# A new hand-written order for a cosFormer attention and token-mixing kernel: most products of v on GpSimd, narrow tiles for k'v, twelve narrow q transposes

## The chip, the cores and the metric

The kernel runs on one core of one Trainium2 chip. Its metric is the device time of one execution, in microseconds (us); lower is better. TensorE multiplies matrices, VectorE, ScalarE and GpSimd work on elements, and SyncE's queue issues the transfers here. Each engine takes its own instructions strictly in order and waits on semaphores for the others.

## What is computed

Two stages, one behind the other, on 8 batches of 576 tokens with 8 heads of 64 columns. First a linear attention with cosine weights:

```python
theta = pi / 2 * pos / S
phi(x) = concat([relu(x) * cos(theta), relu(x) * sin(theta)])      # 64 -> 128 features
kv  = phi(k)^T v            # per head, 128 x 64
z   = sum over s of phi(k)
out = (phi(q) kv) / (phi(q) z + 1e-6)
```

Then, with the eight heads side by side as x (8 x 576 x 512), a mixing over tokens:

```python
wq, wk = x @ w_q, x @ w_k                # 512 -> 64
W_tok  = (wq wk^T) / sqrt(64)            # never built: wk^T x is formed first
result = relu(W_tok x) @ w_out           # 512 x 512
```

Inputs and the result are float32; the kernel works in bfloat16 and sums in float32. In and out are some 39 MB.

## The kernel before

The work is cut into 16 units H = 0 to 15, each a batch and half of its heads (four heads, two per row of 128 partitions); the four heads come as two halves "a" and "b". A batch b holds the units 2b and 2b+1, and a pair of batches fills nine output tiles of 128 rows, 36 tiles in all. The order of all work is one string of words, ORDER, which is read from left to right. Each word issues the instructions of one step on its engine; so for each engine the string fixes the order of its queue, and nothing else does. A letter behind @ names the engine (A ScalarE, V VectorE, G GpSimd), a number behind the colon the PSUM bank (of OE's tile also the output buffer).

The steps of one unit, with the lines of the profile:

- LK, LQ, LV (L145): load half a unit of k, q or v, 288 KB, into one of five raw buffers each.
- RK, RQ (L203, L205): relu of k and q to bfloat16, by halves or whole.
- The products of v with the two tables cos and sin, into one of two buffers "v2". There are two ways: CV (L209, L211), a cast of v to bfloat16 on any engine, and then VS (L234), the product on VectorE from SBUF; or VG (L248), the product on GpSimd straight from the raw float32.
- KV (k'v): per unit 36 matmuls on narrow tiles (L285: 64 rows, 64 columns of weights, 130 moving columns) or, for the units in KV_WIDE, 18 on wide ones (L275: 128 columns of weights, 260 moving). KE evicts the result.
- QT: the transposes of q, 9 wide ones of 128x128 (L295) for the units in QT_WIDE, else 18 narrow ones (L301). QM is the product of q with the tables on VectorE from PSUM: two instructions for a wide unit (L316), one for a narrow one (L320).
- N (L340): numerator and denominator, two steps per unit. EP adds 1e-6 to the denominator on ScalarE or VectorE (L357, L359); for the steps in EPS_PE two small matmuls do it (L348). RC or RJ is the reciprocal, X (L393) the division on VectorE.
- XT (L406, wide) or XR (L419, narrow): transposes of x; XE evicts them.

Then per batch WK, WQ, KX (L439, L452, L466) with their evictions KW, QW, XK, the copies XA and XB across partitions, four MX (L489) and ME (the relu, L500 or L502); per output tile WO (L509, four matmuls), OE (eviction to one of 16 buffers, L209 or L213) and ST (the store, L519). LW and CW load and cast the weights, WU is a few matmuls on constants.

Of the kernel before, what the change touches and what calls it, by code (L numbers as in the profile page):

```python
# [31 lines left out]
RC6 LQ4a KX0:4 X6 RK2@A QT2:2 RC7 X7 CV5@A KV2:0 LK7a XK0@V LV4a QM2 XB0@G QW0@A XT3:6 LV4b KE2@A
RK5@A LK4a VS5a N5:0 WU5:2 LK4b N4:2 VS5b XE3@A RQ5@G LV7a EP5@V KV5:4 RC5 RC4 X5 XA0@A LV7b X4
QT5:6 KE5@A RQ4@G LQ7b MX0:0 QM5 XR2:2 ME0@A LQ7a QT4:4 XE2@A LQ6a N10:0 QM4 MX1:6 CV4@G LK7b EP10@A
ME1@A WK1:2 LV6b WQ1:3 RC10 KW1@A VS4 RK4@A LQ6b KX1:2 MX2:6 LW2 N11:4 XK1@V QW1@A ME2@A EP11@V
KV4:2 LK6b RC11 XA1@G X10 CV7a@A CV7b@G LK6a X11 MX5:6 MX4:0 KE4@A RQ7b@G LV6a RQ7a@A VS7 N8:2 N9:4
ME5@A LV8a ME4@A QT7:6 RK7@G LW3 EP8@V EP9@V RJ4 RQ6a@A XT5:0 X8 LW4 XB1@G XE5@A X9 KV7:2 LW5 RQ6b@G
# [12 lines left out]
MX15:2 EP23@A KX4:5 RK10@A LV13b WQ4:0 XK4@V RQ13b@G RC23 WO3:1 ME15@A X23 XA4@G XB4@A QW4@A RQ12b@G  # L50
KV10:2 OE3:9@V RQ12a@A QT13:6 OE12:10@A VG12 MX18:0 WO14:5 QM13 KE10@A ST12 ME18@A LK13b XR11:2
OE14:11@A LK13a MX16:0 N21:6 XE11@V ME16@A LV14a N20:4 EP21@A EP20@V RK12@A QT12:0 RJ10 X21 WO16:2
RQ14b@A X20 WO13:3 QM12 VG13 XR10:4 OE13:10@A MX19:6 KV12:0 ME19@A ST13 WO17:3 OE16:12@A LK15b
KE12@V XE10@V LK14b MX17:0 LK14a OE17:13@A N25:6 ME17@V N24:4 LV15b RQ14a@A WK5:3 ST2 EP25@V EP24@V
RK13@A RJ12 QT14:0 X24 WO21:2 KW5@A X25 CV14a@G KV13:4 OE21:10@A QM14 CV14b@A WQ5:3 ST21 KE13@A
KX5:2 LQ15b VS14 LQ15a XR12:4 XK5@A N27:0 ST3 XE12@A N26:6 LK15a RK14a@G WO20:2 RC26 EP27@V RC27
XA5@G RK14b@A X27 WO19:4 XB5@G QW5@A VG15b X26 KV14:0 OE19:2@A MX21:6 KE14@A MX23:4 WO18:3 ME21@V
ME23@A OE20:10@V XR13:4 RQ15a@G MX22:6 RQ15b@V MX20:0 ST20 ME22@A WO15:2 VG15a ST17 XE13@V ME20@A
ST8 N28:6 OE18:9@V OE15:14@A ST9 N29:0 EP28@A QT15:4 RK15@A EP29@V RC28 WK6:3 RC29 X29 WO25:2 KW6@A
QM15 WQ6:3 OE25:15@A KV15:0 X28 QW6@A ST25 ST7 KX6:3 KE15@A ST15 N31:0 ST18 XR14:6 EP31@V N30:4 ST0  # L60
XE14@V WO23:2 EP30@A ST10 XK6@A RJ15 ST16 X30 XA6@G WO24:3 ST5 OE23:7@A XB6@G X31 WO26:2 OE24:0@A
# [9 lines left out]
def kernel(  # L71
# [126 lines left out]
    A, V, G = nc.scalar, nc.vector, nc.gpsimd  # L198
# [8 lines left out]
    def cast(eng, dst, s):  # L207
        if eng is A:
            A.copy(dst, s)  # L209
        elif eng is G:  # L210
            G.tensor_scalar(dst, s, 1.0, 1.0, op0=ALU.mult, op1=ALU.mult)  # L211
        else:
            V.tensor_copy(dst, s)  # L213
# [90 lines left out]
    def KE(H, ps, eng):  # L304
        if H in KV_WIDE:
            cast(eng, kv_b[H % 2][:, :, :, :, 0:D + 1],
                 kv_wide(place["KV", H]).rearrange("p r (q s e) -> p r q s e", q=2, s=2))
            return
        cast(eng, kv_b[H % 2][:, :, 0, :, 0:D + 1],
             kv_view(place["KV", H]).rearrange("p r (s e) -> p r s e", s=2))  # L310

    def QM(H, ps, eng):
        if H in QT_WIDE:
            q_t = qt_wide(place["QT", H]).rearrange("p c (r d) -> p r c d", r=2)
            for r in range(2):
                V.tensor_mul(  # L316
                    qm_b[H % NQM][:, :, r, 0:C, :],
                    q_t[:, r].unsqueeze(1).to_broadcast([P, 2, C, H2]), qtab)
# [13 lines left out]
    def N(g, ps, eng):  # L332
# [3 lines left out]
        for u in range(SC):  # L336
            for s in range(2):
                for pr in range(2):
                    a = slice(H2 * pr, H2 * pr + H2)
                    nc.tensor.matmul(  # L340
                        nv[:, pr, u, :], qm_b[H % NQM][a, s, r, 2 * u:2 * u + 2, :],
                        kv_b[H % 2][a, r, pr if H in KV_WIDE else 0, s, 0:D + 1],
                        start=(u == 0 and s == 0),
                        stop=(u == SC - 1 and s == 1 and g not in EPS_PE))
        if g in EPS_PE:
            for pr in range(2):
# [4 lines left out]
    def rec(g):  # L351
        return rec_b[g // 2 % 4][:, g % 2]
# [24 lines left out]
    def RC(g, ps, eng):  # L377
        V.reciprocal(rec(g), num(place["N", g])[:, :, :, D:D + 1] if g in EPS_PE else rec(g))

# [219 lines left out]
```

## Time and profile before

| | |
|---|---|
| median of three runs | 120.03 us (119.75 to 120.36) |
| profiled execution, first to last instruction (span) | 117.9 us |
| TensorE busy | 96.3 us, 82% |
| VectorE busy | 91.0 us, 77% |
| ScalarE busy | 82.7 us, 70% |
| GpSimd busy | 64.8 us, 55% |
| transfers | 39.38 MB, mean 334 GB/s |
| granted TensorE clock | 0.997 |

The profiled execution's own time is not given beside its span; the median of the runs lies 2.1 us above the span, which is what starts and ends around the first and last instruction. The engines' busy times are sums over stages with different limits. Matmuls are pipelined, so how long a step of TensorE keeps the queue is read from the distance of two starts or from the chain of waits rather than from its duration.

### The profile page before, as it was taken

The numbers are of one execution on the slowest core, as the hardware profiler recorded it, in microseconds if no ns is written. First come the engines' busy times: TensorE is split into PE (matmuls) and PEld (weight loads), VectorE is DVE, ScalarE is ACT, GpSimd is POOL, SyncE is SP. The second block draws the span as 40 slices with busy tenths as digits, with TensorE's granted clock in tenths as the row PEclk, the third lists the DMA queues.
The fourth block names the chain that finished last, engine by engine and source line by source line (L and its number), as shares of the span: only waits on it lengthen the run. The fifth ranks groups of instructions, "written<-read, shape, count | busy, mean of one in ns | idle before, by whom it ended". The sixth has DMA issues, their size and how long they took to land.

```text
span 117.9 us, 4967 instructions
## 1 busy us (share of the span) xinstructions
PE 96.3 (82%) x2109; PEld 65.3 (55%) x2109; DVE 91.0 (77%) x163; ACT 82.7 (70%) x146; POOL 64.8 (55%) x66
## 2 busy tenths in 40 slices
PE   0007866887897879998999889997999999999970
PEld 0006855756676768546966556654784566463420
DVE  2009799699899998989798887796997996794620
ACT  4555578489999797997684769975888783546340
POOL 7600599843435984584599972899549921102000
PEclk9999999999999999999999999999999999999998
DMA  3999999999999999999999899786989456999874
GB/s 95 353 389 408 393 363 351 391 389 396 385 393 389 391 385 387 389 395 384 387 381 341 271 317 379 274 253 215 299 285 321 171 205 268 402 343 402 340 306 172
DMA packets 20662, 39.38 MB, mean 334 GB/s; under 512 B 3232, under 2 KB 3232, under 8 KB 20640
## 3 DMA queue, kind: packets, MB, share of 16 engines
q1 hardware_dynamic: 20640, 39.07, 91.8%
q8 instruction: 16, 0.26, 1.0%
q14 instruction: 6, 0.05, 0.1%
HBM read 29.62 MB, written 9.44 MB: 331 GB/s over the span
## 4 chain that ended last, share of the span: by engine, by line
PE 46%; DMA 25%; DVE 9%; SPq 8%; ACT 4%; issue 3%; POOL 2%; POOLq 0%; DVEq 0%
PE ps L509 23%; DMA kraw<-in_k_dram 11%; DMA vraw<-in_v_dram 9%; SPq L145 8%; DMA qraw<-in_q_dram 5%; DVE qm L316 5%; PE ps L340 4%; PE ps L452 3%; PE ps L466 3%; PE ps L489 3%; PE ps L439 3%; PE ps L285 3%; PE ps L419 2%; PE ps L295 2%; POOL rq L205 2%
## 5 line engine op out<-in xcount | busy, mean ns | idle before, releaser
L248 POOL TENSOR_TENSOR v<-vraw,vtab 128x1152 bf16<-128x1152 f32 (+1 forms) x12 | 35.6, 2976 | 4.5 <-DVE qm L316 2.5
L509 PE MATMUL ps<-wow,mix 128*128 128x512 bf16 x144 | 34.6, 380 | 0.0
L393 DVE TENSOR_TENSOR x<-ps,rec 128x640 bf16<-128x640 f32 x32 | 25.4, 816 | 0.7
L209 ACT COPY o<-ps 128x512 f32<-128x512 f32 x25 | 14.6, 590 | 10.5 <-PE ps L509 9.2
L316 DVE TENSOR_TENSOR qm<-ps,qtab 128x1152 bf16<-128x1152 bf16 x28 | 19.7, 749 | 1.3 <-PE ps L295 1.2
L509 PEld LDWEIGHTS <-mix 128*128 128x128 bf16 x144 | 12.5, 98 | 14.5 <-issue 1.7
L295 PE MATMUL ps<-ident,rq 128*128 128x128 bf16 x126 | 10.3, 232 | 10.9 <-ACT rq L203 10.0
L234 DVE TENSOR_TENSOR v<-vb,vtab 128x2304 bf16<-128x2304 bf16 (+1 forms) x11 | 12.0, 1110 | 7.5 <-ACT vb L209 6.7
L500 ACT ACTIVATE mix<-ps 128x576 bf16<-128x576 f32 x23 | 14.5, 651 | 2.5 <-PE ps L489 2.3
L340 PE MATMUL ps<-kvs,qm 64*128 64x65 bf16 x640 | 14.0, 193 | 2.8 <-DVE qm L316 1.8
L340 PEld LDWEIGHTS <-qm 64*128 64x128 bf16 x640 | 12.6, 96 | 4.9 <-issue 3.3
L295 PEld LDWEIGHTS <-rq 128*128 128x128 bf16 x126 | 8.2, 104 | 12.5 <-issue 9.9
L203 ACT ACTIVATE rk<-kraw 128x1152 bf16<-128x1152 f32 (+1 forms) x14 | 13.9, 995 | 0.5 <-DMA kraw<-in_k_dram 0.3
L211 POOL TENSOR_SCALAR kx<-kx 64x256 bf16<-64x256 bf16 x10 | 4.0, 400 | 15.8 <-ACT kx L209 10.1
L205 POOL TENSOR_SCALAR rq<-qraw 128x576 bf16<-128x576 f32 (+1 forms) x13 | 10.1, 776 | 4.4 <-ACT rk L203 2.6
L211 POOL TENSOR_SCALAR vb<-vraw 128x576 bf16<-128x576 f32 (+1 forms) x7 | 5.7, 809 | 10.8 <-DMA vraw<-in_v_dram 9.5
L285 PE MATMUL ps<-v,rk 64*64 64x130 bf16 x432 | 9.1, 228 | 1.9 <-ACT mix L500 0.7
L209 ACT CAST kvs<-ps 128x260 bf16<-128x260 f32 (+1 forms) x15 | 6.5, 436 | 5.1 <-PE ps L285 3.8
L285 PEld LDWEIGHTS <-rk 64*64 64x64 bf16 x432 | 7.5, 112 | 4.3 <-ACT mix L500 1.3
L502 DVE TENSOR_SCALAR mix<-ps 128x576 bf16<-128x576 f32 x9 | 6.8, 753 | 3.3 <-PE ps L489 3.1
L213 DVE COPY xT<-ps 128x1280 bf16<-128x1280 bf16 (+1 forms) x9 | 7.3, 813 | 2.2 <-PE ps L419 2.0
L203 ACT ACTIVATE rq<-qraw 128x576 bf16<-128x576 f32 (+1 forms) x10 | 8.3, 830 | 0.9 <-DMA qraw<-in_q_dram 0.8
(65 smaller groups left out, 135.0 us busy)
## 6 DMA issues: line engine op xcount, KB each, us to landing
kraw<-in_k_dram SPq DMA_DIRECT2D x32, 288.0 KB, 5.9
qraw<-in_q_dram SPq DMA_DIRECT2D x32, 288.0 KB, 5.9
vraw<-in_v_dram SPq DMA_DIRECT2D x32, 288.0 KB, 5.9
out_dram<-o SPq DMA_DIRECT2D x36, 256.0 KB, 3.0
wof<-in_moe_w_out_dram SPq DMA_DIRECT2D x4, 256.0 KB, 5.7
wkf<-in_moe_w_k_dram SPq DMA_DIRECT2D x1, 128.0 KB, 6.7
wqf<-in_moe_w_q_dram SPq DMA_DIRECT2D x1, 128.0 KB, 6.5
```

Source lines behind the costliest of these rows:

```text
L203: A.activation(dst, s, AF.Relu)
L205: eng.tensor_scalar(dst, s, FMAX, 0.0, op0=ALU.min, op1=ALU.max)
L209: A.copy(dst, s)
L234: V.tensor_mul(v2_b[H % NV2][:, part, :, :, 0:D], vb_b[H % NPREP][:, part].unsqueeze(3).to_broadcast([P, n, C, 2, D]), vtab.unsqueeze(1).t ...
L248: G.tensor_mul(dst[:, part, :, :, 0:D], s[:, part].unsqueeze(3).to_broadcast([P, n, C, 2, D]), vtab.unsqueeze(1).to_broadcast([P, n, C, 2, ...
L285: nc.tensor.matmul(kv_v[o, r, :], rk_of(H)[a, pr, c, :], v2_b[H % NV2][a, pr, c, :, 0:D + 1], start=(c == 0), stop=(c == C - 1))
L295: nc.tensor.transpose(qt_v[:, c, :], rq_b[H % NPREP][:, c, :, :], ident)
L316: V.tensor_mul(qm_b[H % NQM][:, :, r, 0:C, :], q_t[:, r].unsqueeze(1).to_broadcast([P, 2, C, H2]), qtab)
L340: nc.tensor.matmul(nv[:, pr, u, :], qm_b[H % NQM][a, s, r, 2 * u:2 * u + 2, :], kv_b[H % 2][a, r, pr if H in KV_WIDE else 0, s, 0:D + 1], ...
L393: V.tensor_tensor(x_b[b % NX][:, :, 4 * h:4 * h + 4, :].rearrange("p u (w r) d -> p r w u d", r=2)[:, r], nv[:, :, :, 0:D], rec(g).to_broa ...
L500: A.activation(dst, s, AF.Relu, scale=scale_moe)
L509: nc.tensor.matmul(o, mix_b[bp % 2][:, m, rt * P:(rt + 1) * P], wow[:, m, :], start=(m == 0), stop=(m == NDM - 1))
```

## The change

The string ORDER is replaced as a whole, and three lists with it. The computation stays as it was. Counted over the kernel:

- products of v: VG goes from 9 half and 3 whole instructions to 21 half and 3 whole; VS from 5 half and 6 whole to 5 half and none. The casts CV go from 9 half and 4 whole to 5 half.
- KV: 72 wide matmuls and 432 narrow ones become 576 narrow ones.
- QT: wide units go from 14 to 4, narrow ones from 2 to 12.
- eps on TensorE: 5 steps become 10.
- relus: GpSimd 18 to 12 instructions, VectorE 4 to 1, ScalarE 24 to 43 (more of them halves).
- evictions move between ScalarE and VectorE in small numbers; loads, stores and output tiles are in another order.

The diff, cut to the lists and the first, a middle and the last lines of the string:

```diff
-LK1b TB TI LQ1a LQ0a TK LV1b TZ LV1a LK1a LQ1b TQ LQ0b LK0a RQ1a@G LV0a TW TV LV0b LK0b CV1@A LV3a
-LV3b VS1b RQ1b@A LQ3b VS1a T2 QT1:0 LQ3a RK1a@A RK1b@V RQ0@V LK3b KV1:2 QM1 LK3a QT0:4 KE1@A CV0@G
...
-OE2:2@A WO4:2 LK11a VS9 OE6:3@A LQ11a RK8b@A QT9:0 RK9a@G OE1:4@A WK3:3 LV11b QM9 QT8:4 RK9b@G KW3@A
-OE4:5@A KV8:0 QM8 XB2@A KV9:6 ST4 KE8@A LV12a MX9:4 KE9@A MX11:0 VG11a N16:2 ME9@A LK10a ME11@V
...
-OE35:4@A ST35 OE31:2@A ST31
+LV1a LV0b TK TQ LV0a TI TZ LV1b LQ1b LQ0a LQ1a LK1a T2 TV TB TW CV1a@A VG0b LK1b CV1b@A LQ0b RK1b@A
+VS1a RQ1@V WU14:0 LW0 RQ0a@A QT1:0 RQ0b@A LK0a LK0b VS1b RK1a@G VG0a KV1:2 QT0:4 LV3a LV2a LQ3a
...
+RQ9a@A QT9:0 OE4:6@A ME8@V RK9a@A QT8:2 RK8a@G KW3@V MX9:4 ME9@A WQ3:7 KX3:6 RK8b@A KV9:4 XK3@A
+KE9@A QM9 KV8:0 N19:4 RQ11b@A QM8 KE8@V N18:2 LV10a N16:0 EP16@V EP18@A EP19@V QW3@A WO7:6 RQ11a@A
...
+XB4@G MX13:4 RC22 ME13@A X22 N23:2 VG13a MX17:0 KE10@V N20:6 WO13:4 ME17@A EP23@V RC23 X23 EP20@V
...
+ST35 OE31:6@V ST32 OE33:10@A ST27 ST33 OE34:13@V ST31 ST34 WO28:6 OE28:0@A ST28
@@
-    EPS_PE = (3, 4, 14, 16, 26)
+    EPS_PE = (0, 1, 4, 5, 8, 9, 10, 14, 15, 25)
-    QT_WIDE = (0, 1, 2, 3, 4, 5, 6, 7, 8, 9, 10, 11, 12, 14)
-    KV_WIDE = (2, 4, 5, 7)
+    QT_WIDE = (0, 1, 2, 3)
+    KV_WIDE = ()
```

GpSimd's queue around the units 8 and 9, before. A row is line, operation, output, inputs and shape; "vraw" is a raw buffer of v, "v_84" and "v_85" the two buffers v2, "rk" and "rq" the relus, "x2" two rows alike (both halves):

```order
L205 TENSOR_SCALAR rq_80<-qraw_71 128x9x64
L205 TENSOR_SCALAR rk_78<-kraw_66 128x576
L205 TENSOR_SCALAR rq_81<-qraw_72 128x9x64 x2
L205 TENSOR_SCALAR rk_79<-kraw_67 128x576 x2
L248 TENSOR_TENSOR v_85<-vraw_74,vtab 128x18x64 x2
L205 TENSOR_SCALAR rq_80<-qraw_68 128x2x9x64
L248 TENSOR_TENSOR v_84<-vraw_73,vtab 128x18x64
```

The same place in the change ("vb" is a cast half of v, "kx" a copy across partitions):

```order
L211 TENSOR_SCALAR vb_83<-vraw_77 128x576
L248 TENSOR_TENSOR v_84<-vraw_76,vtab 128x18x64 x2
L248 TENSOR_TENSOR v_85<-vraw_77,vtab 128x18x64
L205 TENSOR_SCALAR rk_78<-kraw_66 128x576
L248 TENSOR_TENSOR v_85<-vraw_74,vtab 128x18x64 x2
L211 TENSOR_SCALAR kx_103<-kx_103 64x256
```

The relus of q and of pair 9's k have left GpSimd; in front of the one relu that stays (of k of unit 8) three half products of v have come in.

VectorE's queue ahead of the k'v of the units 8 and 9, before:

```order
L234 TENSOR_TENSOR v_84<-vb_82,vtab 128x36x64
L393 TENSOR_TENSOR x_95<-ps,rec_92 128x2x5x64
L502 TENSOR_SCALAR mix_105<-ps 128x576
L213 COPY xT_97<-ps 128x2x2x5x64
L234 TENSOR_TENSOR v_85<-vb_83,vtab 128x36x64
L316 TENSOR_TENSOR qm_87<-ps,qtab 128x2x576 x2
L316 TENSOR_TENSOR qm_86<-ps,qtab 128x2x576 x2
```

and in the change:

```order
L234 TENSOR_TENSOR v_85<-vb_83,vtab 128x18x64
L359 TENSOR_SCALAR rec_92<-ps 128x10 x2
L213 COPY o_107<-ps 128x512
L381 RECIPROCAL rec_92<-rec_92 128x20
L393 TENSOR_TENSOR x_95<-ps,rec_92 128x2x5x64 x2
L213 COPY o_109<-ps 128x512
L213 COPY o_110<-ps 128x512
L213 COPY xT_97<-ps 128x2x2x5x64
L502 TENSOR_SCALAR mix_105<-ps 128x576
L213 CAST wk_99<-ps 128x320
L320 TENSOR_TENSOR qm_87<-ps,qtab 128x4x576
L320 TENSOR_TENSOR qm_86<-ps,qtab 128x4x576
```

The two whole products of v are replaced by one half product, the two products of q per unit by one each, and three evictions of output tiles and one of wk have come in.

GpSimd's queue behind that place, in the change, up to its last product of v:

```order
L211 TENSOR_SCALAR kx_102<-kx_102 64x256 x2
L248 TENSOR_TENSOR v_85<-vraw_76,vtab 128x18x64
L248 TENSOR_TENSOR v_84<-vraw_75,vtab 128x36x64
L205 TENSOR_SCALAR rk_78<-kraw_65 128x576
L248 TENSOR_TENSOR v_85<-vraw_76,vtab 128x18x64
L248 TENSOR_TENSOR v_84<-vraw_77,vtab 128x36x64
L205 TENSOR_SCALAR rq_81<-qraw_68 128x2x9x64
L248 TENSOR_TENSOR v_85<-vraw_73,vtab 128x36x64
```

The two copies of batch 4 now stand ahead of the products for the units 12 to 15.

More of the change, by code (lines that the diff above doesn't have):

```diff
@@ L32 @@
[L32 to L37, printed above, removed]
@@ L50 @@
[L50 to L55, printed above, removed]
@@ L56 @@
[L56 to L61, printed above, removed]
@@ new lines @@
+RC4 VG4a LV7a RC5 LK7b X5 XT3:4 XA0@A XB0@A MX0:2 LQ7b LQ7a LV6b X4 QM5 LW2 LK6b LV6a XE3@V ME0@A
+MX1:6 RK5b@A RK5a@A LK6a XR2:2 MX3:0 ME1@A XE2@V KV5:4 LQ6b RQ4@A RK4b@G LQ6a MX2:6 WK1:2 KE5@A
+ME2@V KW1@V QT4:6 N11:4 LW3 VG7b RK4a@A ME3@A KV4:2 QM4 VG7a EP11@A RC11 N10:0 KE4@A X11 LW4 RC10
+N9:2 RC9 RK7a@A N8:6 RK7b@A RC8 VG6b VG6a KX1:4 WQ1:5 X9 XK1@A XB1@A X8 X10 LW5 XR4:6 LV9a QW1@A
+MX7:4 XR5:0 KV7:2 RQ7@A XA1@A XE4@V QT7:6 KE7@A ME7@A XE5@V MX4:0 RQ6a@G ME4@A WK2:2 QM7 LQ8b CW3@G
+LV8b MX5:4 MX6:0 LK9b KW2@A N14:6 N15:2 ME5@V RK6@A WQ2:4 RC14 CW4@G LV8a X14 LQ9b RQ6b@A KX2:5 RC15
@@ new lines @@
+RC18 OE7:7@A RC19 RC16 X19 VG11b WO12:7 WO0:6 X16 QT11:0 VG11a N17:4 X18 LQ10a XR9:2 XA3@A OE0:8@V
+OE12:9@A RK11b@A WO9:7 LK10a EP17@V RK11a@A LK12b WO11:6 LK10b LV12b RC17 LQ13b X17 KV11:4 QM11
+XB3@G LQ13a XE9@A OE9:10@A KE11@V XR8:2 OE11:11@A XE8@V LQ12b LV13a LV12a RQ10a@A LK13b RQ10b@A
+LQ12a MX15:6 VG10b MX12:0 VG10a WO10:4 WK4:5 LK13a ME12@A ME15@V QT10:6 RK10@G LK12a N22:0 RQ13b@G
+MX14:2 LQ14b OE10:12@A WQ4:4 KW4@A RQ13a@G KX4:5 ME14@A EP22@A QW4@A XK4@A XA4@G ST4 QM10 KV10:6
+XB4@G MX13:4 RC22 ME13@A X22 N23:2 VG13a MX17:0 KE10@V N20:6 WO13:4 ME17@A EP23@V RC23 X23 EP20@V
@@ new lines @@
+N21:0 MX16:2 WO17:5 RC20 EP21@V LQ14a LV13b RK12b@A RQ12b@A OE13:13@A RQ12a@A RC21 WO15:4 X21 ME16@A
+LK14b OE17:14@A XR11:0 X20 XR10:6 MX19:2 OE15:15@A ME19@A WO16:5 XE11@V VG12 QT13:2 QT12:0 RK13a@A
+XE10@V MX18:6 WK5:4 LV14b ST3 OE16:6@V RQ14b@A LV14a LK14a ME18@V RK12a@G QM12 WO19:5 LQ15a KW5@A
+OE19:0@A KV12:6 RQ14a@A LV15b KX5:4 KE12@A WQ5:5 N25:6 QM13 XK5@A RK13b@A QW5@V XB5@A N24:2 XA5@A
+RC25 QT14:4 VG13b ST2 KV13:0 EP24@A X25 KE13@A WO18:6 ST8 LQ15b WO21:7 QM14 N26:4 RC24 N27:0
+OE18:5@A ST10 LV15a ST1 X24 OE21:4@A XR12:2 ST6 LK15b EP26@V EP27@V RK14@A WO20:7 RJ13 XE12@A WO14:6
```

34 lines of the change are left out of this document (17 added, 17 removed).

## The prediction

> **What bounds the kernel now.** I read the stage windows first, then the chain of waits, then the groups of instructions with shapes kept apart. The stage windows (length; busy time of TensorE, its weight loads, VectorE, ScalarE and GpSimd with counts; granted clock; DMA share; GB/s):
>
> ```profile
> 9.60:25.10 15.50, 12.32 (x336) 10.14 (x336) 13.75 (x27) 9.77 (x17) 10.96 (x5) 1.00 1.06 380
> 25.10:56.00 30.90, 27.51 (x595) 20.44 (x596) 28.84 (x51) 27.60 (x48) 17.41 (x21) 1.00 1.05 390
> 56.00:96.70 40.70, 38.91 (x952) 25.62 (x953) 34.98 (x62) 31.15 (x59) 30.82 (x18) 1.00 0.87 297
> 96.70:114.30 17.60, 17.56 (x234) 9.08 (x232) 11.57 (x19) 8.13 (x17) 1.60 (x4) 1.00 0.88 334
> 114.30:117.90 3.60, 0.00 (x0) 0.00 (x0) 0.00 (x0) 0.58 (x1) 0.00 (x0) 0.90 0.52 201
> ```
>
> Up to about 56 us the transfers run at 390 GB/s and VectorE is busy 28.84 of 30.90 us, while GpSimd idles for 13.5. After that TensorE has no gaps worth naming, and the transfers fall to 297 GB/s. The last 3.60 us are one eviction and the last store. So there are two parts: a first one paced by loads and VectorE, a second one paced by TensorE's queue. The chain of waits (start, length, what) shows the seam and the spacing of TensorE's steps:
>
> ```profile
> 45.54 0.65 PE ps L285 x35
> 47.87 2.70 PE ps L509 x12
> 51.77 0.40 PE ps L419 x20
> 54.00 0.52 PE ps L295 x9
> 54.54 2.76 DVE qm L316 x4
> 57.34 0.42 PE ps L489 x4
> 82.59 0.62 PE ps L340 x40
> 83.21 0.69 PE ps L439 x20
> 92.37 0.24 PE ps L489 x4
> 94.31 0.26 PE ps L301 x18
> 96.13 0.61 PE ps L452 x8
> 97.39 0.67 PE ps L466 x10
> 104.93 0.55 PE ps L466 x10
> 114.30 0.58 ACT o L209
> ```
>
> At 54.54 VectorE's products of q for head pairs 9 and 8 hold TensorE; the k'v products of 8 and 9 follow and end at 57.34. I call the moment when both of these k'v are done M. In the profiled execution M is 57.34, and from M to TensorE's end at 114.30 are 56.96 us.
>
> **TensorE behind M.** From the rows a k'v with narrow tiles takes 0.65, nine wide q transposes 0.52, eighteen narrow ones 0.26, one numerator step 0.31 (0.62 for two), XR 0.40, WK 0.69, WQ 0.61, KX 0.61 (mean of 0.67 and 0.55), MX 0.12, one output tile 0.90 (2.70 for three). The additions of eps on TensorE I take at 0.1. Counting the words of the order behind M: before, 30 output tiles, 8 XR, 4 wide and 2 narrow transposes, 6 k'v, 16 numerators, 2 eps, 4 WK, 5 WQ, 5 KX, 23 MX: 27.0+3.2+2.6+3.9+5.0+0.2+2.8+3.1+3.1+2.8 = 53.7. The 56.96 measured are 1.06 times that; the factor is the small stalls. In the change 29 output tiles, 8 XR, 6 narrow transposes, 6 k'v, 16 numerators, 1 eps, 4 WK, 4 WQ, 4 KX, 20 MX: 26.1+3.2+1.6+3.9+5.0+0.1+2.8+2.4+2.4+2.4 = 49.9, times 1.06 is 52.9. That is 4.1 us less behind M, of which 1.1 are the narrow transposes and the rest is work that the new order has put ahead of M.
>
> The four k'v with wide tiles are the other saving on TensorE. Two of its rows give their spacing, 40.86 minus 39.85:
>
> ```profile
> 39.85 1.19 PE L275 MATMUL ps<-v,rk 64*128 64x260 bf16 x18 [0.32 <-DVE x L393]
> 40.86 0.30 PE L489 MATMUL ps<-wq,kx 64*128 64x288 bf16 x2
> ```
>
> Four times 1.01-0.65 is 1.4 us, and six more narrow transposes ahead of M are 1.6; but ahead of M the loads and VectorE set the pace, so I count these 3.0 us as paying for the extra work there (one output tile, WQ, KX, three MX: 2.5 us) and as nothing more. Five more eps additions cost TensorE 0.5 and save five small operations elsewhere.
>
> **When M comes.** The groups, with shapes apart (busy, mean ns), and three rows on GpSimd and VectorE in order of time:
>
> ```profile
> L248 POOL TENSOR_TENSOR v<-vraw,vtab 128x1152 bf16<-128x1152 f32 x9 | 21.9, 2433 | 3.0 <-DVE qm L316 2.5 <-DMA vraw<-in_v_dram 0.4
> L248 POOL TENSOR_TENSOR v<-vraw,vtab 128x2304 bf16<-128x2304 f32 x3 | 13.8, 4604 | 1.5 <-PE ps L348 1.1 <-PE ps L285 0.4
> L234 DVE TENSOR_TENSOR v<-vb,vtab 128x2304 bf16<-128x2304 bf16 x6 | 8.4, 1406 | 0.7 <-POOL vb L211 0.7
> L205 POOL TENSOR_SCALAR rq<-qraw 128x576 bf16<-128x576 f32 x10 | 6.6, 665 | 1.2 <-DMA qraw<-in_q_dram 0.7 <-PE ps L509 0.2
> L205 POOL TENSOR_SCALAR rk<-kraw 128x576 bf16<-128x576 f32 x4 | 4.2, 1062 | 4.6 <-DMA kraw<-in_k_dram 4.6
> L234 DVE TENSOR_TENSOR v<-vb,vtab 128x1152 bf16<-128x1152 bf16 x5 | 3.6, 754 | 6.8 <-ACT vb L209 6.7
> L213 DVE COPY o<-ps 128x512 f32<-128x512 f32 x11 | 7.5, 685 | 1.6 <-PE ps L509 1.6
> L502 DVE TENSOR_SCALAR mix<-ps 128x576 bf16<-128x576 f32 x9 | 6.8, 753 | 3.3 <-PE ps L489 3.1
> L213 DVE COPY xT<-ps 128x1280 bf16<-128x1280 bf16 x8 | 6.6, 820 | 2.1 <-PE ps L419 2.0
> L205 POOL TENSOR_SCALAR rq<-qraw 128x1152 bf16<-128x1152 f32 x3 | 3.4, 1146 | 3.2 <-ACT rk L203 2.6 <-ACT kx L209 0.4 <-DMA qraw<-in_q_dram 0.2
> L211 POOL TENSOR_SCALAR kx<-kx 64x256 bf16<-64x256 bf16 x10 | 4.0, 400 | 15.8 <-ACT kx L209 10.1 <-DVE rec L378 2.4 <-DVE rec L359 1.9
> 52.08 0.66 POOL L205 TENSOR_SCALAR rk<-kraw 128x576 bf16<-128x576 f32 x1
> 52.95 1.35 DVE L234 TENSOR_TENSOR v<-vb,vtab 128x2304 bf16<-128x2304 bf16 x1
> 53.61 1.21 POOL L205 TENSOR_SCALAR rk<-kraw 128x576 bf16<-128x576 f32 x1 [0.87 <-DMA kraw<-in_k_dram]
> ```
>
> Three bounds on M. Loads: before, the half of k that starts GpSimd at 53.61 is the sixtieth half load, with all six weight loads ahead of it. In the change the sixtieth is again the last that M needs (a half of k of pair 8), with the same weights ahead. At the same rate it lands at 53.6; its relu on GpSimd takes 0.66, and one k'v 0.65, so M cannot be before 55.0, 2.3 us sooner. VectorE: ahead of M the order takes away five whole products of v (5 x 1.41 = 7.0 us), one product of q (1.4, half of the 2.76 for two) and some 2.1 us of small ones, 10.5 in all; it gives VectorE three more xT (2.5), three outputs (2.1), two mix (1.5) and three small casts (1.3), 7.4. The net is some 3 us less of the 42.6 between 9.6 and 56 us, so VectorE alone would allow M at about 54.3. GpSimd: 15 half products ahead of M, 15 x 2.43 = 36.5 us, where it had three halves and one whole (11.9), and nine relus and casts at 0.66, 6 us, and small ones, 2: some 44.5 us. Begun when the first v has landed at about 5 us, that ends at 49.5 if GpSimd never waits; with the loads spaced 0.76 us (288 KB at 390 GB/s) I find it never more than one half product behind a landing, so the load of 53.6 still decides.
>
> Before, M came 3.7 us behind that landing; the least is 1.4. I take 2.6, M at 56.2, because between the k'v of pair 2 and those of pair 8, a stretch of 30.9 us before (25.1 to 56.0), all five queues now hold 27 to 29 us of work by these means (transfers, GpSimd, VectorE, ScalarE, TensorE), where GpSimd had 17.4: small waits remain. The ends are 55.0 and 60.0 (one and a half times the old lag, 3.7, behind the landing, with 0.9 for an output tile in front).
>
> **Contention.** GpSimd's relu of 53.61 took 1.21 in place of 0.66: it ended 0.52 behind VectorE's product of 52.95. Over the four such relus of k that is 4 x (1.06-0.67) = 1.6 us. So keeping the two apart gives back at most 1.6 us, on an engine that idles; I count it as nothing. The Trainium skill, "SBUF — State Buffer", section "Who interferes with whom", says that a VectorE instruction with two SBUF inputs and a GpSimd one that reads SBUF exclude each other for a whole instruction, whichever starts first; the row agrees. What matters is the other direction: should VectorE wait in that way for a GpSimd product, it would lose up to that product's length, 2.43 us. The change has five VectorE products left and four casts or relus between SBUF tiles, and only the order keeps them apart, no wait does.
>
> **GpSimd behind M.** Behind the relu of pair 8, done at 54.3, it has six half and three whole products (14.6+13.8), two whole and three half relus (2.3+2.0) and three copies (1.2), 33.9 us up to its last product. One wait stands in its queue: the copies XA4 and XB4 need KX4, which TensorE reaches 11.2 us of spacings behind M, about 56.2+11.9 = 68.1, and a cast behind it (0.4). GpSimd would be there at 66.9; from 68.5 it has 0.8 for the two copies and 20.5 for what follows, so its last product of v ends at 89.8. TensorE reaches the last k'v, 32.4 us of spacings behind M, at 56.2+34.4 = 90.6. So the cover is under 1 us; each further microsecond that GpSimd loses is lost at the end, since TensorE's queue goes in order and behind that k'v stand 17 us of work. A half of v now costs 2.43 on GpSimd where a cast of 0.67 and VectorE's 0.75 did it. The Trainium skill, "GPSIMD Engine Reference", section "4.1 Engine selection", advises against this move, GpSimd being some 2x slower for two-input operations; here it is 3.2x against VectorE's product. By that rule the second rival, 119, would be the outcome.
>
> **The rest.** The stores between the loads hold the load queue in the profile (row below, the last load); in the change nine stores stand between them, of tiles evicted long before, so the last half of k lands near 53.6+36x0.76+9x0.68 = 87.1, 3.5 us ahead of its k'v. ScalarE's sum hardly changes (fewer whole relus, more halves). Start and tail stay: the first transposes wait for the relu of the seventh load (8.75 us) in both, and 3.6 us lie behind TensorE's end.
>
> ```profile
> 8.77 0.68 ACT L203 ACTIVATE rq<-qraw 128x576 bf16<-128x576 f32 x1 [0.22 <-DMA qraw<-in_q_dram]
> 9.60 1.12 PE L295 MATMUL ps<-ident,rq 128*128 128x128 bf16 x9 [9.60 <-ACT rq L203]
> 88.87 0.43 SPq L145 DMA_DIRECT2D kraw<-in_k_dram  x1
> ```
>
> **Sum.** 56.2+52.9+3.6 = 112.7 span, against 117.9. The runs' median, 120.03, lies 2.1 above that span, so the time is 114.8; I say 115.0.
>
> **Rivals.** (1) M is not earlier, 57.3 to 60, because the loads pace that part and five full queues get in each other's way: 57.3+52.9+3.6+2.1 = 115.9, to 118.6; I name 117. For it: the DMA share of 1.05 in that stage; against it: the 3.7 us lag. (2) GpSimd becomes the bound behind M: 17 instructions that lose 0.3 us each, 5 us, less the cover of 0.8 put the last k'v 4 us late and the time at 119: same or just faster. For it: 33.9 us of work and a wait in 35; against it: the products' mean of 2433 ns, beside a relu that once lost 0.5. (3) Slower: VectorE's products drift into GpSimd's and wait. M must then come after 62.0 (120.6-2.1-3.6-52.9), 7.0 us later than its bound; three blocked products of 2.4 us do it, 7.2, and the time would be 121 to 123. For it: 15 GpSimd products stand ahead of M; against it: the eleven products that VectorE had kept means of 1406 and 754 ns, so they hardly met GpSimd. (4) The change doesn't do what it says, the conflicts it removes being 1.6 us on an idle engine: that is so, but the work behind M falls all the same, so it ends as rival 1.
>
> **Chances.** Forecast 0.53 (own range 112.8 to 116.5), rival 1 0.16, rival 2 0.13, rival 3 0.17, still better than the forecast 0.01. A change under 0.5% can't be told from none. Faster: 0.53+0.16+0.01 and 0.04 of rival 2, 0.74; same: 0.08 of rival 2; slower: 0.17 and 0.01 of rival 2, 0.18. The range 112.8 to 120.6 leaves out most of rival 3 and little below.
>
> **What would show it.** Right: the second of k'v 8 and 9 ends at 55 to 57.5; GpSimd busy about 84 us, with products at 2.4; TensorE without gaps from there, ending near 109; the last k'v at 90 to 91. Wrong: VectorE products above 1 us, TensorE waiting for GpSimd's v behind 70 us, a last product of v behind 92, or loads that wait for raw buffers ahead of 50 us.

## The result, and the profile after

The change makes the kernel slower: 125.81 us (median of four runs, 125.62 to 126.19) against 120.06 (119.75 to 120.36) for the kernel before, a ratio of 1.047 with a 95% interval of 1.043 to 1.050. Forecast were 115.0 us, so the sign is wrong. The profiled execution took 126.19 us, its span is 124.4. A few executions of some kernels below took over 1.5% longer than the fastest of the same kernel, and the medians and ratios leave these out.

From the page of the changed kernel: the engines' busy time; in 40 equal slices the clock granted to TensorE and the rate of the transfers; and the queue that brings instructions (packets, MB, share of the transfer engines' time):

```profile
PE 96.4 (77%) x2293; PEld 63.0 (51%) x2293; DVE 89.3 (72%) x154; ACT 82.3 (66%) x152; POOL 82.0 (66%) x63
...
PEclk9999999958999999999999779999999999999999
...
GB/s 113 350 377 367 375 393 376 376 390 390 391 389 389 375 392 382 391 387 391 388 391 391 398 387 277 260 366 404 193 5 90 115 395 94 75 404 285 346 322 93
...
q8 instruction: 18, 0.29, 0.9%
```

TensorE carries out 2293 matmuls where it had 2109, and is busy as long as before (96.4 against 96.3). The clock is lower in the slices of two places, at 25 to 31 and at 68 to 75 us, where it had stayed whole.

The stage windows, cut at the first transposes, at the k'v of unit 2, at the moment M when both k'v of 8 and 9 are done, at 104.20, and at TensorE's end (columns as in the prediction):

```profile
10.80:25.10 14.30, 10.62 (x288) 8.80 (x289) 12.06 (x21) 8.70 (x16) 13.33 (x9) 1.00 1.05 380
25.10:64.45 39.35, 31.38 (x888) 22.25 (x888) 31.23 (x49) 28.59 (x56) 29.67 (x19) 0.96 1.05 388
64.45:104.20 39.75, 37.46 (x967) 23.92 (x965) 31.66 (x59) 31.35 (x59) 32.76 (x17) 0.96 0.75 271
104.20:120.00 15.80, 15.76 (x153) 7.69 (x153) 10.60 (x19) 7.86 (x15) 0.40 (x1) 1.00 0.67 257
120.00:124.40 4.40, 0.00 (x0) 0.00 (x0) 0.00 (x0) 0.58 (x1) 0.00 (x0) 1.00 0.43 164
```

In the second stage no engine is near full: TensorE 31.38 of 39.35 us, VectorE 31.23, ScalarE 28.59, GpSimd 29.67. M lies where the numerators follow the two k'v (TensorE in order of time):

```profile
63.22 1.25 PE L285 MATMUL ps<-v,rk 64*64 64x130 bf16 x72
64.45 1.10 PE L340 MATMUL ps<-kvs,qm 64*128 64x65 bf16 x60
```

So M is 64.45 and not 56.2, from M to TensorE's end it is 55.5 us and not 52.9, and the tail 4.4 and not 3.6: 8.25 + 2.6 + 0.8 = 11.7 us, the whole difference between the span of 124.4 and the 112.7 of the forecast.

**Where TensorE stood still.** Its rows around the four longest gaps:

```profile
37.74 0.36 PE L340 MATMUL ps<-kvs,qm 64*128 64x65 bf16 x11
40.47 0.33 PE L340 MATMUL ps<-kvs,qm 64*128 64x65 bf16 x9 [2.37 <-issue]
...
48.39 0.71 PE L466 MATMUL ps<-x,wk 128*64 128x256 bf16 x9
49.85 0.30 PE L466 MATMUL ps<-x,wk 128*64 128x256 bf16 x1 [0.75 <-issue]
...
54.09 0.59 PE L509 MATMUL ps<-wow,mix 128*128 128x512 bf16 x2
55.99 1.25 PE L509 MATMUL ps<-wow,mix 128*128 128x512 bf16 x5 [1.31 <-issue]
...
65.49 1.47 PE L509 MATMUL ps<-wow,mix 128*128 128x512 bf16 x6
68.94 1.49 PE L509 MATMUL ps<-wow,mix 128*128 128x512 bf16 x5 [1.98 <-issue]
```

Each gap lies in the middle of a step: eleven matmuls of a numerator run, then nothing for 2.37 us, then the other nine, on the same tiles. So a wait for another engine is unlikely, and the profile names none ("issue"). Counted from the start, 606, 862, 989 and 1245 matmuls lie ahead of these gaps, which leave 94, 94, 93 and 93 when divided by 128. With its weight load a matmul is two instructions, so every gap stands at a multiple of 256 instructions plus nearly the same offset; I call these places the ends of 256. The trace also records the transfers of instructions: 18 packets of 16 KB, as many as TensorE passes such ends (16 and 16 before). Put side by side, in us:

```
end of 256 passed   next packet starts   first matmul behind the next end   gap there
34.8                37.9                 40.47                              2.37
40.47               42.5                 44.75                              none
44.75               47.7                 49.85                              0.75
49.85               53.5                 55.99                              1.31
55.99               59.8                 63.5                               none
63.5                66.5                 68.94                              1.98
```

In this table a packet starts 2.0 to 3.8 us after TensorE has passed such an end (median 3.0 between 25 and 80 us), and where TensorE stands, it goes on 2.2 to 2.6 us after the start of the packet. Two smaller gaps ahead of the table, at 21.4 and 29.0 us, also end 2.6 us behind the start of a packet. Where the 256 instructions in between last longer than these two times together, some 5.5 us, nothing is seen; where they last less, TensorE stands. The second stretch of the table, 4.3 us, is just long enough, because its packet came after 2.0. I call this theory F (instruction fetch). The 0.29 MB and 0.9% of the page's row give no hint of it.

### The profile page after: what moved, and what is told of

Same layout as the page of the kernel before. It is cut to its first block, busy times and chain, and to the rows that moved or that the text cites. A ratio compares the mean times of both kernels' runs of the same rounds, so it can differ in the third digit from the quotient of the medians.

```text
span 124.4 us, 5320 instructions
## 1 busy us (share of the span) xinstructions
PE 96.4 (77%) x2293; PEld 63.0 (51%) x2293; DVE 89.3 (72%) x154; ACT 82.3 (66%) x152; POOL 82.0 (66%) x63
## 5 line engine op out<-in xcount | busy, mean ns | idle before, releaser
L248 POOL TENSOR_TENSOR v<-vraw,vtab 128x1152 bf16<-128x1152 f32 (+1 forms) x24 | 64.0, 2689 | 5.8 <-DMA kraw<-in_k_dram 4.0
L203 ACT ACTIVATE rq<-qraw 128x576 bf16<-128x576 f32 (+1 forms) x21 | 15.5, 752 | 3.8 <-DMA qraw<-in_q_dram 3.3
L203 ACT ACTIVATE rk<-kraw 128x576 bf16<-128x576 f32 (+1 forms) x22 | 15.5, 726 | 3.5 <-DMA kraw<-in_k_dram 3.4
L320 DVE TENSOR_TENSOR qm<-ps,qtab 128x2304 bf16<-128x2304 bf16 x12 | 16.0, 1347 | 2.3 <-PE ps L301 2.2
L213 DVE COPY o<-ps 128x512 f32<-128x512 f32 x12 | 8.2, 688 | 5.5 <-PE ps L509 5.4
L295 PE MATMUL ps<-ident,rq 128*128 128x128 bf16 x36 | 3.6, 265 | 10.0 <-DVE rq L205 8.2
L234 DVE TENSOR_TENSOR v<-vb,vtab 128x1152 bf16<-128x1152 bf16 x5 | 7.0, 1398 | 3.5 <-ACT vb L209 3.5
L205 POOL TENSOR_SCALAR rk<-kraw 128x576 bf16<-128x576 f32 (+1 forms) x7 | 5.7, 819 | 4.2 <-DMA kraw<-in_k_dram 3.8
L295 PEld LDWEIGHTS <-rq 128*128 128x128 bf16 x36 | 2.8, 120 | 11.2 <-DVE rq L205 8.9
L489 PE MATMUL ps<-wq,kx 64*128 64x288 bf16 x64 | 8.2, 287 | 0.1
```

The costliest lines, as they stand in the source:

```text
L203: A.activation(dst, s, AF.Relu)
L248: G.tensor_mul(dst[:, part, :, :, 0:D], s[:, part].unsqueeze(3).to_broadcast([P, n, C, 2, D]), vtab.unsqueeze(1).to_broadcast([P, n, C, 2, ...
L320: V.tensor_mul(qm_b[H % NQM][:, :, :, 0:C, :].rearrange("p s r c d -> p s r (c d)"), qt_view(place["QT", H]).unsqueeze(1).to_broadcast([P, ...
L489: nc.tensor.matmul(pair(ps)[:, t, :].bitcast(FP32)[:, 0:HS], kx_b[b % 2][a, (m // 2) ^ t, (m % 2) * P:(m % 2 + 1) * P], wq_b[b % 2][a, :], ...
```

## The experiments

Rivals of F were L (VectorE's products of v are held by GpSimd's, the third rival of the prediction) and O (the new order makes engines wait for each other, whatever the tiles). The trace shows such a hold. VectorE and GpSimd in the changed kernel, ahead of M:

```profile
51.27 1.36 DVE L320 TENSOR_TENSOR qm<-ps,qtab 128x2304 bf16<-128x2304 bf16 x1 [1.21 <-PE ps L301]
52.55 2.28 DVE L234 TENSOR_TENSOR v<-vb,vtab 128x1152 bf16<-128x1152 bf16 x1
```

```profile
51.84 7.55 POOL L248 TENSOR_TENSOR v<-vraw,vtab 128x1152 bf16<-128x1152 f32 x3
59.47 0.67 POOL L205 TENSOR_SCALAR rk<-kraw 128x576 bf16<-128x576 f32 x1
```

The half product took 2.28 us where 0.754 was the mean before, beside GpSimd's three products. Below, "gaps" is the sum over the ends of 256 instructions of the longest distance between two matmuls there, where it is over 0.35 us, each less 0.1: 0.9 us for the kernel before, 8.5 after. Such a sum also takes in waits of another kind that happen to lie at an end. I call "fetch gaps" the part in which TensorE goes on within 2.7 us of a packet's start: none before, all 8.5 after.

**Tile widths of before in the new order.**

```diff
-    QT_WIDE = (0, 1, 2, 3)
-    KV_WIDE = ()
+    QT_WIDE = (0, 1, 2, 3, 4, 5, 6, 7, 8, 9, 10, 11, 12, 14)
+    KV_WIDE = (2, 4, 5, 7)
```

> The order and the GpSimd products of the change, with the tile widths of before (QT_WIDE and KV_WIDE), so 184 fewer matmuls in TensorE's queue (2109 as before). Theory F (instruction fetch): TensorE's gaps in the middle of a step, 7.3 us in all after the change, fall below 2.5 us, since its instructions pass more slowly; the second of k'v 8 and 9 ends at 58 to 61 in place of 64.5, and the time is 119.5 to 122.5, although the wide tiles cost TensorE 3 us of work. Rival L (VectorE's products held by GpSimd's): the widths do not matter to that; the k'v still ends at 63 to 65 and the time is 124.5 to 127. Rival O (the new order itself is worse and the narrow tiles were a saving): 126 to 129.

Measured: 123.15 us (1.023 times before, 1.017 to 1.029), M at 62.2, gaps 3.7, of them fetch gaps 2.4. The widths take away 162 matmuls (2131 are left) and not all 184. So more work on TensorE, in fewer instructions, makes the kernel 2.7 us faster; L and O fall as sole causes. Time, M and gaps all came out above what F had expected: a gap of 2.1 us at 64 is left.

**The narrow tiles in the old order.** The same two lists, the other way round, in the kernel before.

> The order of the kernel before, with the tile widths of the change, so only 184 more matmuls, each of the narrow steps shorter. Theory F: TensorE gets gaps of 0.5 to 2.5 us in the middle of steps ahead of 75 us, at matmul numbers equal to 93 to 99 modulo 128, 2 to 5 us in all; the time is 121 to 125. Rivals L and O (locks, or the order): no such gaps; the 3 us of TensorE work saved bring 0 to 2 us, the time is 118 to 120.

Measured: 122.56 us (1.014, 1.006 to 1.022), gaps 3.8, of them fetch gaps 1.9. The narrow tiles alone turn the old order slower, as F says.

**The program moved by 61 matmuls.**

```diff
-VS1a RQ1@V WU14:0 LW0 ...
+VS1a RQ1@V WU258:0 LW0 ...
-    WARM_COLS = 384
+    WARM_COLS = 128
```

> The changed kernel with 64 warming matmuls at the start in place of 3 (narrower ones, 128 columns), in the time in which TensorE waits for the first half of q; its whole program stands 61 matmuls later in the queue. Theory F: the gaps in the middle of steps stay at the same matmul numbers modulo 128 (93 to 95), so they move 61 matmuls of program earlier, to other steps; about 5 to 8 us in all. If they belong to the steps (rivals L and O: a wait for an operand, that the profile does not name), they stay with the steps, so at numbers modulo 128 of 26 to 28. Time 123 to 127 by both.

The gaps over 1.5 us in TensorE's rows:

```profile
42.41 0.56 PE L452 MATMUL ps<-xT,wqw 128*64 128x288 bf16 x6 [1.55 <-issue]
52.38 0.44 PE L419 MATMUL ps<-ident,x 64*128 64x64 bf16 x9 [2.25 <-issue]
67.87 1.04 PE L340 MATMUL ps<-kvs,qm 64*128 64x65 bf16 x55 [2.03 <-issue]
```

They stand behind 734, 989 and 1245 matmuls, which leave 94, 93 and 93 divided by 128, and in other steps of the program than before (WQ, XR and N in place of N, KX and WO). The gaps keep to the count and not to the step: nothing that a step waits for can do that. Time 127.79 us, gaps 7.9, of them fetch gaps 6.5. It is 2.0 us longer than the changed kernel; the granted clock was lower (0.90 and 0.91 in its two executions against 0.94 to 0.97), which may be why.

**Without the loads from the sixth unit on.**

```diff
-            nc.sync.dma_start(raw[nm][H % NRAW][:, r, :], src[nm][b][:, 2 * h + r, :])
+            if H < NRAW:
+                nc.sync.dma_start(raw[nm][H % NRAW][:, r, :], src[nm][b][:, 2 * h + r, :])
```

> The changed kernel without the loads of q, k and v from the sixth unit on: the raw buffers keep old data, so the output is not the reference's; the instructions of TensorE and their order stay. Theory F: with the transfer engines free the next 256 instructions come in time; no gap above 0.3 us in the middle of a step from 45 us on, and these gaps sum to under 1.5 us. If the gaps belong to the steps, those at 54 to 69 us (3.3 us) are still there at the same matmuls. The time falls to 105 to 118 in any case, since what waited for loads runs sooner.

TensorE's waits without a releaser, first in the changed kernel and then here, where the same lines stand one further down (total, times, longest):

```profile
PE ps L509 <- issue: 3.3, 2, 2.0
PE ps L340 <- issue: 2.6, 2, 2.4
...
PE ps L466 <- issue: 0.7, 1, 0.7
```

```profile
PE ps L341 <- issue: 0.2, 1, 0.2
PE ps L510 <- issue: 0.2, 1, 0.2
```

The same instructions in the same order, and the gaps are gone (0.7 us in all): they come with the loads. The one execution took 118.59 us, just above the expected range.

**The held product and the late start.** The first kernel leaves out the held VectorE product (CV9a and VS9a); the second loads unit 1 first, and VG0b moves behind the relu of k:

```diff
-LV1a LV0b TK TQ LV0a TI TZ LV1b LQ1b LQ0a LQ1a LK1a T2 TV TB TW CV1a@A VG0b LK1b CV1b@A LQ0b RK1b@A
-VS1a RQ1@V WU14:0 LW0 RQ0a@A QT1:0 RQ0b@A LK0a LK0b VS1b RK1a@G VG0a KV1:2 QT0:4 LV3a LV2a LQ3a
+LV1a LK1b TK TQ LV1b TI TZ LQ1b LQ1a LK1a LV0b LQ0a LV0a T2 TV TB TW CV1a@A LQ0b CV1b@A RK1b@A
+VS1a VS1b RQ1@V WU14:0 LW0 RQ0a@A QT1:0 RQ0b@A LK0a LK0b RK1a@G VG0b VG0a KV1:2 QT0:4 LV3a LV2a LQ3a
```

> The changed kernel without the cast and VectorE's product of half a of unit 9's v (that half keeps an older unit's values, so the output is not the reference's): the one VectorE product that stood behind GpSimd's at 52.55 us and took 2.28 in place of 0.75. Theory L (such waits are a good part of the loss): the second of k'v 8 and 9 ends 1.5 to 2.3 us earlier than 64.5, the time falls by as much, to 123.5 to 124.3. Theory F (TensorE is held by its instructions ahead of that place): under 1 us, 124.8 to 126.

> The changed kernel with the loads of unit 1's k and q moved ahead of unit 0's v, and GpSimd's first product of v behind its relu of k: the first transposes start at 8.6 to 9.6 us instead of 10.8, the first k'v at 10 to 10.7 instead of 12.0. If the late start is passed on to the end, the time falls by 1 to 1.5 us, to 124.3 to 124.8. Theory F: TensorE's later steps then run into the next 256 instructions just as early, so that part or all of it goes into longer gaps: 125 to 126.

Measured: 125.40 and 125.67 us, against 125.81. In the second the first k'v began at 9.7 us in place of 12.0, and M was still 64.6. This gain was gone by the second end of 256, at 21.7 us against 21.4, and not in a gap there: TensorE waited longer for relus of q (2.9 us against 1.0 by then), and its clock was 0.82 from 10 to 25 us where it had been 1.00. F had expected longer gaps, but they fell to 6.4. From 40 to 56 us both kernels pass the four ends at times that differ by 0.6 us at most, each 2.2 to 2.6 us behind the start of a packet. So neither the held product nor the start set the time. L is no cause of the time worth naming, though the hold itself is real (2.28 us in place of 0.75).

**Wide k'v for 8 and 9, and a candidate.** Both on the new order with the widths of before and wide k'v for 8 and 9. The candidate also has the start above, puts the copy XB2 on ScalarE and moves VS9a back:

```diff
-    KV_WIDE = (2, 4, 5, 7)
+    KV_WIDE = (2, 4, 5, 7, 8, 9)
-... XB2@G LK9a CV9a@G ... N12:2 VS9a N13:0 ... RK8a@G KW3@V
+... XB2@A LK9a CV9a@G ... N12:2 N13:0 ... RK8a@G KW3@V VS9a
```

> The order of the change with the tile widths of before, and also wide k'v for the units 8 and 9: 36 fewer matmuls just ahead of the gap of 2.1 us at 63.7 to 65.8 that was left there, for 0.7 us more of TensorE work. Theory F: that gap falls under 0.8 us, the time from 123.15 to 121.8 to 122.8. Without F: 0.7 us more, 123.5 to 124.

> All together, as a candidate: the order of the change, the tile widths of before and wide k'v for 8 and 9, the start with unit 1's loads first, the copy of batch 2 on ScalarE, so that GpSimd does not wait for it, and VectorE's product of unit 9 behind the work on x, where GpSimd has nearly done. If fetch, start and locks are the whole loss, they give back 1.3 + 1.2 + 1.5 of the 3.1 us that are left against before: 119 to 120.5. If the order itself is slower for another reason: 121 to 123.

Measured: 122.21 us with gaps of 1.2, none of them fetch gaps, as F expects (the gap at 64 us is gone, for 0.7 us more of work); and 121.90 for the candidate (1.012 times before, 1.005 to 1.018), whose VectorE products all took 0.75 us and whose first k'v began at 9.4. Its gaps grew to 3.1, of them fetch gaps 1.9, so here TensorE waited for instructions again. Fetch, start and holds taken out were expected to give 119 to 120.5 if they were the whole loss; by this run they are not, though fetch gaps remained in it. The kernel without fetch gaps is still 1.014 times before (1.005 to 1.022); 0.7 us of that is the added work, and where the rest comes from was not separated.

**Narrow tiles only where the loads thin out.** On the kernel before, on the new order, and on the candidate:

```diff
-    QT_WIDE = (0, 1, 2, 3, 4, 5, 6, 7, 8, 9, 10, 11, 12, 14)
+    QT_WIDE = (0, 1, 2, 3, 4, 5, 6, 7, 8, 9)
```

and, in the second of the four, also unit 7:

```diff
-    KV_WIDE = (2, 4, 5, 7)
+    KV_WIDE = (2, 4, 5)
```

> The kernel before with narrow q transposes for the units 10, 11, 12 and 14 only, behind the moment of the k'v of 8 and 9; 36 more matmuls, 4 x (0.52 - 0.26) = 1.0 us less of TensorE work. Theory F: there the loads thin out, no gap above 0.5 us opens at the ends of the 256 instructions, and the time falls by 0.3 to 1.0 us, to 119.4 to 120.2 beside 120.4. If narrow tiles are no saving anywhere: 120.4 to 121.5.

> The same, and narrow k'v for unit 7, whose 256 instructions lasted 7.5 us before (37.8 to 45.3), the longest of all: 18 more matmuls for 0.36 us less of TensorE work. Theory F: a block with slack can take them, no new gap there, the time 0 to 0.4 us under the previous one; 119.0 to 120.2. Otherwise at or above the kernel before, 120.4 to 121.5.

> The order of the change with wide k'v for 2, 4, 5 and 7 and wide q transposes up to unit 9, as before, and narrow ones from unit 10 on, as in the change. Against the run with all widths of before (123.15) 36 more matmuls behind 75 us. Theory F: 122 to 123.2, the gaps ahead of M as there (2.1 us at 64 too). If the narrow transposes cause the gaps wherever they stand: 123.5 to 125.

> The candidate (wide k'v also for 8 and 9, unit 1's loads first, the copy and VectorE's product moved) with narrow q transposes from unit 10 on. Theory F: 1.0 us less TensorE work where the loads thin out, 121 to 122 beside 122.2; gaps at the ends of the 256 instructions together 2 to 3.5 us as there. It is not expected to beat the kernel before.

Measured: 120.75 (1.005, 1.002 to 1.008), 122.37 (1.018, 1.014 to 1.022), 122.56 and 123.53 us. All but the third expectation failed. In the first there are no fetch gaps, TensorE works 1.0 us less behind M, and its idle time there grows by more than that: behind M the old order has no use for a faster TensorE. The fourth is 1.6 us slower than the candidate although its fetch gaps are no larger (1.6), so F does not explain it, and its cause stays open. The second is the plainest case of F. One k'v on narrow tiles, 18 more matmuls, costs 1.6 us against the first, and a fetch gap of 1.5 us has opened:

```profile
47.27 0.42 PE L419 MATMUL ps<-ident,x 64*128 64x64 bf16 x18
49.15 0.20 PE L419 MATMUL ps<-ident,x 64*128 64x64 bf16 x2 [1.45 <-issue]
```

The slack that I had read off one stretch of 256 instructions (37.8 to 45.3) was not there to be used: the 18 matmuls moved the ends, the next stretch began at 44.3 and was through at 47.7, and the packet behind it had started only at 46.6.

**Both orders with both widths, without the loads.** The edit is that of the run without the loads, on four kernels.

> The kernel before without the loads of q, k and v from the sixth unit on (old data, the output is not the reference's). It gives the base for the three below: 114 to 118, since the waits for loads behind 20 us fall away.

> The order of before with the narrow tiles of the change, without those loads. With the loads the narrow tiles cost 2.1 us in this order (122.56 against 120.43). Theory F: without the loads the instructions come in time, and the narrow tiles are the saving that they were counted as: 1 to 3 us under the kernel before without the loads. If narrow tiles cost time for another reason: 1 to 3 us above it.

> The order of the change with the tile widths of before, without those loads. With the loads this order costs 2.7 us (123.15 against 120.43). If that is fetch and loads alone: within 1 us of the kernel before without the loads. If the order is slower by its waits between engines: 2 to 4 us above it.

> The changed kernel without those loads, once more (118.59 in one look): 118 to 119. Theory F: 1 to 3 us under the same order with the wide tiles; with the loads it was 2.7 us above it.

Medians in us:

| | with the loads | without the loads from the sixth unit on |
|---|---|---|
| old order, widths of before | 120.06 | 120.68 |
| old order, narrow tiles | 122.56 | 120.57 |
| new order, widths of before | 123.15 | 120.44 |
| new order, narrow tiles (the change) | 125.81 | 117.26 |

Without the loads the change is 3.4 us faster than the kernel before without them (its ratio to the kernel before with loads is 0.982, 0.972 to 0.993, from three executions); with them it is 5.8 slower. Each half alone is worth nothing without the loads, and together they are worth 3.4. My reading, which no run separates, is that the order gives TensorE the work in time and the narrow tiles shorten it. With the loads the narrow tiles alone cost 2.1 and the order alone 2.7 (the kernel before ran at 120.43 beside them), and both together 5.8. The kernel before does not run faster without its loads (1.003, 0.999 to 1.007): they were not its pace. So two expectations failed here by over 1 us: the kernel before was to gain 2 us or more, and the narrow tiles in the old order 1 to 3. The k'v of 8 and 9 without the loads, in the old order and in the new, whose ends are M (58.7 and 58.9, next to 57.34 and 64.45 with the loads):

```profile
57.33 1.24 PE L286 MATMUL ps<-v,rk 64*64 64x130 bf16 x72 [0.43 <-DVE qm L317]
```

```profile
57.64 1.24 PE L286 MATMUL ps<-v,rk 64*64 64x130 bf16 x72
```

and the new order with narrow tiles behind M, up to TensorE's end:

```profile
58.87:111.05 52.18, 51.70 (x1118) 30.84 (x1114) 42.25 (x78) 39.11 (x73) 33.17 (x18) 1.00 0.41 154
```

Here the packets of instructions start 1.0 us (median, 25 to 80 us) behind the ends, where with the loads it was 3.0.

**Fewer loads in flight.** In the trace the issue of a load waits until the transfer eight before it has landed, and a load takes 5.8 us to land. So a transfer of 64 bytes behind each load halves the loads in flight; the second kernel is the control.

```diff
+            if H >= 2:
+                slot = thr_n[0] % 16
+                thr_n[0] += 1
+                nc.sync.dma_start(scr[0:1, slot, :], src[nm][b][0:1, 0, 0:16])
```

> The changed kernel with a transfer of 64 bytes issued behind each load from the third unit on. Eight transfers are in flight at most in the trace (each waits for the one eight before it), so now only four loads are, and a load's 5.8 us from issue to landing should fall to some 3 to 4. Theory F with a queue (the fetch of instructions lies behind the loads in flight): fetches come 2 to 3 us sooner, the gaps at the ends of the 256 instructions fall from 8.5 us to under 3, and the time to 118 to 121.5, if four loads in flight still keep 360 to 390 GB/s. If the fetch is slow for another reason: gaps of 7 us or more, 125 to 127; if the loads become the bound: 124 to 130 with GB/s below 340.

> The same small transfers in the kernel before, as control: its gaps are 0.9 us in all, so theory F gives nothing to win: 119.5 to 121; loads that become the bound: 121 to 125.

Measured: 140.14 and 136.82 us, far above every expectation. The loads became the bound, in the first kernel mostly at 250 to 300 GB/s where they had run at 390:

```profile
GB/s 147 296 388 376 341 226 304 283 278 289 268 286 281 319 256 365 259 294 288 291 282 248 276 245 300 272 314 297 309 214 254 344 316 373 102 257 404 212 364 129
```

The packets of instructions now start 0.9 us (median, 25 to 80 us) behind the ends of 256, so with fewer loads in flight the fetch does come sooner. The gaps are 3.8 us, of them fetch gaps 0.9; in the control they rose from 0.9 to 6.5, none of them fetch gaps, so these are waits for the loads. That speaks for a fetch that queues behind the loads, but the lower rate may have done the same, and the time can't tell. What exactly holds the packet back stays open, and so does whether a kernel can have the one without the other. No version beat the kernel before.

## Why the prediction was wrong, point by point

**The step that failed** is the price of the narrow tiles. The prediction took "four times 1.01-0.65 is 1.4 us, and six more narrow transposes ahead of M are 1.6" as TensorE work saved, "paying for the extra work there", and never counted instructions: 184 more matmuls (162 of them from the narrow tiles), 368 more instructions, which pass in half the time each or less. In place of a saving the narrow tiles cost 2.1 us in the old order and 2.7 in the new (123.15 to 125.81), and brought the fetch gaps from 2.4 to 8.5 us. During the loads TensorE needs some 5.5 us for every 256 (3.0 in the median until the packet starts, 2.2 to 2.6 until it can be used), or 43 ns per matmul, an estimate from these two rows of times. By the prediction's own rows a narrow k'v takes 0.65 us for 36 matmuls, 18 ns each, and a wide one 1.01 for 18, 56 ns. The kernel before passed its ends every 5.2 to 7.2 us between 26 and 69, without a fetch gap: there was little room for faster instructions.

**M at 56.2.** Measured 64.45. The three bounds (loads 55.0, VectorE 54.3, GpSimd 49.5 and a little) left out the one that decided, TensorE itself and its instructions. Without the loads M is 58.9, 2.7 later than forecast. There TensorE's row of the two k'v above shows no wait, and from 39.8 us to M its rows have one wait, of 0.2 us (second row below). VectorE's product at the same place was held for 2.54 as well, but was done at 50.4:

```profile
47.89 2.54 DVE L235 TENSOR_TENSOR v<-vb,vtab 128x1152 bf16<-128x1152 bf16 x1
```

```profile
54.20 1.02 PE L510 MATMUL ps<-wow,mix 128*128 128x512 bf16 x4 [0.20 <-DVE o L214]
```

So these 2.7 us are TensorE's own work ahead of M and what it lost ahead of 39.8, the start 1.2 us late among it; the shares weren't separated. The other 5.6 us come with the loads, and the gaps at the ends of 256 ahead of M sum to 6.0 (0.3 without the loads).

**"A first one paced by loads and VectorE".** The loads were not the pace: the kernel before without them has M at 58.7 and takes 120.68. TensorE, busy 27.5 of 30.9 us in that stage, had little room for the 2.5 us of work that the order moves ahead of M, and the narrow tiles did not pay for it. Without the loads the change has M at 58.9, within the first rival's 57.3 to 60, and takes 117.26 beside its 117: with instructions in time the kernel comes out as that rival has it, "M is not earlier".

**Behind M 52.9.** The count of steps was right: 52.2 without the loads. With them 55.5. One gap of 1.98 and a stretch of lowered clock behind it (0.96 over 39.75 us, an estimate of up to 1.6 us) about make up the difference.

**Contention "counted as nothing".** Right for the time, though not for the rows: VectorE's five half products had a mean of 1.4 us in place of 0.75, and taking the worst away changed the time by 0.4 us. The third rival gave the right sign, with M after 62.0, and a time of 121 to 123 that falls short of 125.8; its hold was there, but did not set the time, so its right sign was luck.

**GpSimd behind M.** Its last product ended at 101.3 and not at 89.8, with M 8.25 later and 3.6 us of waiting for KX's eviction; behind 70 us TensorE's matmuls never waited for GpSimd, and once a weight load did, for 0.6 us. The second rival did not come in.

**The start.** "Stays" was wrong by 1.2 us (first transposes at 10.80 and not 9.60), and did not matter: the run that mended it had lost the gain by 21.7 us and ended at the same time.

The Trainium skill, "Runtime: NRT & Kernel Launch", section "Instruction fetch mechanics", says that the sequencer fetches the next 256 instructions through its own DMA queue while it carries out the present ones, and that crossing such a boundary is mostly hidden. The trace agrees on the 256 and on the queue; it was hidden in the kernel before (no fetch gap) and nearly so in the change without the loads (0.7 us of gaps), but not in the change with them (8.5 us of gaps).

## What to carry to other kernels

Before replacing matmuls by more and shorter ones, count TensorE's instructions and divide the run into stretches of 256: while transfers run at full rate, a stretch must last longer than the fetch of the next (some 5.5 us here), or the saving comes back as a gap. A gap in the middle of a step with no releaser, whose instruction number leaves the same rest each time, is the sign, and moving the program by some instructions tells it from a wait. Test which resource sets a stage by taking it away (here: the loads) before the forecast leans on it.

## What the runs showed of the hardware

- TensorE takes its instructions in packets of 16 KB, 256 instructions: 18 packets for the 4586 instructions of 2293 matmuls. A packet starts 3.0 us (median, 25 to 80 us) after TensorE has passed the end of 256 while loads run at 390 GB/s, and 1.0 us after it without loads; where TensorE stands, it goes on 2.2 to 2.6 us after that.
- A packet takes about 1 us itself in both cases (0.9 to 1.4), so the loads delay its start, not its transfer.
- In these programs a transfer waits for the one eight before it, so one of 64 bytes between the loads takes a place among the eight in flight: the rate fell from 388 to 286 GB/s.
- The granted clock was 0.96 in both long stages after, where it had been 1.00. At 69.8 us it was halved for 3.4 us, 0.9 us behind the end of a stall; behind the stalls that ended at 40.5, 49.9 and 56.0 it stayed whole, so the runs don't show that a stall brings it down.
